# A Fourier filter and soft mixture of experts on one core: the first DFT stage with its operands swapped, its result kept in SBUF

## The chip, the core and the metric

The kernel runs on one core of one Trainium2 chip. A core has TensorE (PE in the profile; its weight loads are shown apart as PEld), VectorE (DVE), ScalarE (ACT), GpSimd (POOL) and SyncE (SP), whose queue here issues every DMA. The metric is the device time of one execution in microseconds (us). Before the change three runs took 440.77, 441.68 and 442.54 us, a median of 441.68 us. The profiled execution took 440.74 us; its span from the first to the last instruction of the program is 439.0 us.

## The reference

The input `x` holds 8 batches of 2496 rows of 256 float32 values. Each column of a batch is filtered in frequency, and all 19968 filtered rows then go through a soft mixture of 8 experts with 4 slots each. Cut to what is computed:

```python
X = np.fft.rfft(x, axis=1)
Y = X * (filt_r + 1j * filt_i)[None]
x = np.fft.irfft(Y, n=x.shape[1], axis=1).reshape(-1, 256)
logits = x @ phi                                  # 19968 x 32
d = softmax of logits down the columns            # over all rows
slot_input = d.T @ x                              # 32 x 256, 4 rows per expert
slot_out = relu(slot_input[e] @ w1[e]) @ w2[e]    # for each of the 8 experts
c = softmax of logits along the rows              # over the 32 slots
out = c @ slot_out                                # 19968 x 256
```

## The kernel before

A batch's DFT over 2496 = 39 x 64 points is done in two matrix stages. Row number s is written as 64 s1 + s2. The **first stage** sums over the 39 values of s1 with a small cosine and sine matrix `w1q`; three values of s2 share one matmul, so that 3 x 39 = 117 partitions are contracted and 3 x 40 = 120 numbers come out (20 residues t, a real and an imaginary part each). The **second stage** sums, for each t, over the 64 values of s2 and the two parts, 128 terms in all, and gives 64 frequencies.

*The first stage* (`s1_unit`, L271) holds `w1q` still in the array and streams the data past it, 512 columns (two groups of s2 by 256 columns of x) at a time, 11 units in a batch. For batch 0 that is one float32 matmul (L278). For the others `split_x` (L258) has ACT round the data to a short float32r value `xh` (L267) and POOL compute the remainder `xl` (L268), and three float32r matmuls replace the float32 one (L281): w1h by xh, w1l by xh, w1h by xl. The result has (j, q) on its partitions, but the second stage needs (s2, part) there. So ACT (DVE for some units of batch 0) copies it to `at` (L285, L283), a DMA writes it to `a_dram` in DRAM (L289), and `load_ash` (L299) reads it back in the other arrangement, 256 KB for two values of t.

*The second stage* (`x_unit`, L305) handles two values of t in one slot, 10 slots in a batch, 80 in all. It makes four matmuls with `ash` as the operand that stays, 128 rows by 128 columns, and 128 streamed columns of the table `b_t` (L312). DVE multiplies the result by the real and by the imaginary filter (L325, L326), DVE or POOL adds (L328), POOL subtracts (L329). `t_unit` (L333), two slots later, transposes the products on PE (L339) for ACT to copy into a `y` tile (L341). Every second slot it also multiplies by phi: eight matmuls with 32 columns of weights each, four of them standing side by side in the four column quarters of the array (L350).

*The rest.* After each group of batches (0 and 1, 2 and 3, 4 and 5, 6, 7) a `chain` (L363) computes the logits (an inverse DFT of the filtered products with phi, L383 to L430), their running maximum, the dispatch weights and their DFT (L461 to L527), and adds to the slot inputs with matmuls over the saved `y` tiles (L554). It is a Python generator, advanced by `hop`, two steps in each slot, and its matmuls, too, often use 32 columns in quarters of the array. After the last group come `psi` (L777), the experts (L789 to L815), and the output stage (L832 to L913), which scales and transposes the combine weights, multiplies them by the slot outputs and writes 20 MB to DRAM.

*What sets the order.* Each engine runs its own instructions in program order. The order in each engine's program is made at build time by a list scheduler from the order in which the code issues the work: in slot n the second stage of that slot, the first stage of units five slots ahead (`AHEAD`), the transposes of two slots back, two hops. All loads, the writes to `a_dram` among them, stand in SP's one queue. The order of the loads at the start is written by hand (`STEPS`, L59).

*PSUM* is eight banks of 2 KB per partition: two each for the first stage (`ps_s1`), the second (`ps_x`), the transposes (`ps_t`) and the chain (`ps_c`).

Of the kernel before, what the change touches and what calls it, by code (L numbers as in the profile page):

```python
# [19 lines left out]
NT = 20  # L20
NI = 22
NH = 11
PK = 3
KR = PK * N1
# [11 lines left out]
NSPILL = 2  # L36
OUT_ORDER = (4, 5, 0, 1, 2, 3, 6, 7)
# [3 lines left out]
XC = 4  # L41
XB = 3
AB = 5
AHEAD = 5
ASH = 5
LT = 2
HOPS = 2
RT = 1
PR = 2
FB = 1  # L50
WM = 3
MV = 4
PA = 6
YB = 34
WL = 5
SB = 2


STEPS = "IB P FC TC TC TC C XC C XC CC AA X - - - ATATAT"  # L59
# [19 lines left out]
def shape_constants():  # L79
# [27 lines left out]
    bm = bm.reshape(P, NT, P)  # L107
    be = np.zeros((2, N2, 2, 2, 2, 32))
    for h in range(2):
        sg = 1.0 if h == 0 else -1.0  # L110
        for m in range(32):
            ph = 2 * np.pi * (((m + h) * s2) % N2) / N2
            co, si = np.cos(ph), np.sin(ph)
            be[0, :, 0, 0, h, m] = co
            be[0, :, 0, 1, h, m] = -si
            be[0, :, 1, 0, h, m] = sg * si
            be[0, :, 1, 1, h, m] = sg * co
            be[1, :, 0, 0, h, m] = -sg * si
            be[1, :, 0, 1, h, m] = -sg * co
            be[1, :, 1, 0, h, m] = co  # L120
            be[1, :, 1, 1, h, m] = -si
    tw = 2 * np.pi * np.repeat(s2, 2)[:, None] * np.arange(NT)[None] / SEQ
    bt = np.concatenate([bm[:, 0], be[0].reshape(P, P), be[1].reshape(P, P), np.cos(tw), np.sin(tw)], axis=1)
    for t in range(1, NT):
        full = be[0].reshape(P, P) * np.cos(tw[:, t : t + 1]) + be[1].reshape(P, P) * np.sin(tw[:, t : t + 1])
        assert np.abs(full - bm[:, t]).max() < 1e-12
    bh = bm[:, 0, :].copy()
# [51 lines left out]
def filter_layout(filt, special_zero):  # L179

    idx = np.array([[[freq_of(t, h, m) or 0 for m in range(32)] for h in range(2)] for t in range(NT)])
    a = filt[idx.reshape(NT, 64)]
    a = np.ascontiguousarray(a.reshape(NT, 64, 2, P).transpose(3, 0, 2, 1))
    if special_zero:
        a[:, 0, :, 0] = 0
    return a.reshape(P, NT * 2 * 64)
# [3 lines left out]
def fft_soft_moe(ctx, tc, x, fr, fi, fny, phi, w1, w2, cst, w1q, bmat, out):  # L190
# [5 lines left out]
    ps_s1 = ctx.enter_context(tc.tile_pool(name="ps_s1", bufs=2, space=PSUM))  # L196
    ps_x = ctx.enter_context(tc.tile_pool(name="ps_x", bufs=2, space=PSUM))
    ps_t = ctx.enter_context(tc.tile_pool(name="ps_t", bufs=2, space=PSUM))
    ps_c = ctx.enter_context(tc.tile_pool(name="ps_c", bufs=2, space=PSUM))
# [3 lines left out]
    w1h = const.tile([KR, QP], F32R, name="w1h")  # L203
    w1l = const.tile([KR, QP], F32R, name="w1l")
    nc.vector.tensor_copy(w1h, w1q_t)
    nc.vector.tensor_tensor(out=w1l, in0=w1q_t, in1=w1h.bitcast(F32), op=ALU.subtract)

    cst_t = const.tile([P, CST.shape[1]], F32, name="cst_t")
    b_t = const.tile([P, NT, P], F32, name="b_t")
# [22 lines left out]
    x0_cm, x0p = open_pool("x0p", 6, "left")  # L232
    tabs_cm, tabs = open_pool("tabs", 1, "right")
    prod_cm, prod = open_pool("prod", 2, "right")
    proda_cm, proda = open_pool("proda", 3, "right")

    fr_t = tabs.tile([P, NT, 2, 64], F32, name="fr_t")
    fi_t = tabs.tile([P, NT, 2, 64], F32, name="fi_t")

    xv = x.rearrange("b (s1 s2) d -> b s1 s2 d", s2=N2)  # L240
# [3 lines left out]
    def load_x(b, c):  # L244
        pool = x0p if b == 0 else proda
        t = pool.tile([KR, XC, DIM], F32, tag="xt", name=f"xt{b}_{c}", bufs=6 if b == 0 else XB)
        i0 = c * XC
        n = min(XC, NI - i0)
        for j in range(PK):
            s0 = run_of(i0, j)  # L250
            sp.dma_start(t[j * N1 : (j + 1) * N1, 0:n, :], xv[b, :, s0 : s0 + n, :])
        xts[b, c] = t

    a_dram = {}

    xhl = {}

    def split_x(b, u):  # L258

        c, k = divmod(2 * u, XC)  # L260
        xs = xts[b, c][:, k : k + 2, :]
        if b < FB:
            xhl[b, u] = xs, None
            return
        xh = proda.tile([KR, 2, DIM], F32R, tag="xh", name=f"xh{b}_{u}", bufs=3)
        xl = proda.tile([KR, 2, DIM], F32R, tag="xl", name=f"xl{b}_{u}", bufs=3)
        act.copy(xh, xs)  # L267
        pool_e.tensor_tensor(out=xl, in0=xs, in1=xh.bitcast(F32), op=ALU.subtract)  # L268
        xhl[b, u] = xh, xl

    def s1_unit(b, u):  # L271
        if u == 0:
            a_dram[b] = scr.tile([N2, QR, DIM], F32, tag="a_dram", name=f"a_dram{b}")
        xh, xl = xhl.pop((b, u))
        ps = ps_s1.tile([QP, 2, DIM], F32, tag="s1", name=f"s1_{b}_{u}")
        at = proda.tile([QP, 2, DIM], F32, tag="at", name=f"at{b}_{u}", bufs=AB)
        if xl is None:
            pe.matmul(ps, w1q_t, xh, start=True, stop=True)  # L278
        else:
            for n, (w, xx) in enumerate(((w1h, xh), (w1l, xh), (w1h, xl))):  # L280
                pe.matmul(ps, w, xx, start=(n == 0), stop=(n == 2))  # L281
        if b == 0 and u % 2 == 1:
            dve.tensor_copy(at, ps)  # L283
        else:
            act.copy(at, ps)  # L285
        k0 = PK * 2 * u
        dma = sp.dma_start
        if u < NH - 1:
            dma(a_dram[b][k0 : k0 + 2 * PK].rearrange("(i j) q d -> (j q) i d", j=PK), at)  # L289
        else:  # L290
            dma(a_dram[b][k0 : k0 + PK].rearrange("j q d -> (j q) d"), at[:, 0, :])
            dma(a_dram[b][k0 + PK], at[0:QR, 1, :])
# [4 lines left out]
    ashs = {}  # L297

    def load_ash(b, c):  # L299
        t0 = 2 * c  # L300
        ash = prod.tile([P, 2, DIM], F32, tag="ash", name=f"ash{b}_{c}", bufs=ASH)
        sp.dma_start(ash, a_dram[b].rearrange("k (r t) d -> (k r) t d", t=NT)[:, t0 : t0 + 2, :])
        ashs[b, c] = ash

    def x_unit(b, c):  # L305

        t0 = 2 * c
        ash = ashs.pop((b, c))
        ps = ps_x.tile([P, 4, 2, 64], F32, tag="x", name=f"x_{b}_{c}")
        for k in range(2):  # L310
            for dh in range(2):
                pe.matmul(  # L312
                    ps[:, 2 * k + dh].rearrange("q r c -> q (r c)"),
                    ash[:, k, dh * P : (dh + 1) * P],
                    b_t[:, t0 + k, :],
                    start=True,
                    stop=True,
                )
        frv = fr_t[:, t0 : t0 + 2].rearrange("q p h (o c) -> q (p h) o c", o=1).broadcast_to([P, 4, 2, 64])
        fiv = fi_t[:, t0 : t0 + 2].rearrange("q p h (o c) -> q (p h) o c", o=1).broadcast_to([P, 4, 2, 64])  # L320
# [9 lines left out]
        if c == 0:  # L330
            dve.tensor_tensor(out=yt[:, 0:2, 1, 0], in0=ps[:, 0:2, 1, 0], in1=fny_t, op=ALU.mult)
# [302 lines left out]
    for c in range(6):  # L634
        load_x(0, c)
# [310 lines left out]
```

## Time and profile before

| what | value |
|---|---|
| median of three runs | 441.68 us (440.77 to 442.54) |
| profiled execution, its span | 440.74 us, 439.0 us |
| first and last matmul of the second stage (L312) | 35.4 us, 300.4 us |
| `psi`, with which the experts begin (L777) | 349.0 us |
| first output matmul, last output matmul (L885) | 371.7 us, 430.7 us |
| bytes moved by DMA | 107.01 MB |
| of these, `a_dram` written and read back | 21.0 MB and 21.0 MB |
| mean granted TensorE clock | 0.975 |

A row of a group names line, engine, operation, output and inputs, shapes and count; then the time during which at least one instruction of it ran, the mean of one in ns, and the idle time of the engine ahead of them. A row of the timeline gives the start, the length from first start to last end, and the count of like instructions. Matmuls overlap, so the pace of TensorE is the distance between starts, not the length. A float32 matmul of 128 columns stands in the trace as two instructions, each with a weight load; a transpose is one. A row by stretch of time gives the busy time of PE, PEld, DVE, ACT and POOL, then the granted clock, the share of the DMA engines and GB/s.

### The profile page before, as it was taken

Reading aid. Unit: us, or ns where it says so; the run is one execution under the profiler, and the core shown is the slowest. Engines: PE = TensorE matmul, PEld = TensorE weight load, DVE = VectorE, ACT = ScalarE, POOL = GpSimd, SP = SyncE. Lnnn points to the kernel's source line nnn. Section 1 sums busy time; section 2 is a strip of 40 time slices with the busy share of each in tenths; the row PEclk is TensorE's granted clock in tenths of the full one; section 3 lists DMA queues with packets and bytes.
Section 4 is the critical chain, followed back from the end, with each engine's and each line's share of the span. In section 5 each row is a group of like instructions: output and inputs, shape, how many; then the busy total and the mean of one; then the engine's idle time right before and its main releaser. Section 6 shows DMA issues by size and latency. Waiting matters only on the chain. (4 is left out here: it accounts for less than half of the span.)

```text
span 439.0 us, 12271 instructions
## 1 busy us (share of the span) xinstructions
PE 383.8 (87%) x4705; PEld 293.1 (67%) x4705; DVE 288.8 (66%) x571; ACT 235.9 (54%) x513; POOL 232.7 (53%) x290
## 2 busy tenths in 40 slices
PE   8658788897999899999998999999999699878882
PEld 3236565685978687887877688777767445667761
DVE  1336442794699983878999287896477324777882
ACT  2376546466676845775693333461454122766772
POOL 0029557687769564966876056572200103877880
PEclk9879999999999999999999999999998999998997
DMA  6999999989979969787995624332298992787897
GB/s 172 258 274 268 299 277 294 316 253 307 296 230 312 288 194 297 223 260 210 264 293 168 218 76 121 97 99 97 80 375 295 298 283 94 293 341 301 320 352 262
DMA packets 62683, 107.01 MB, mean 244 GB/s; under 512 B 7006, under 2 KB 38622, under 8 KB 61090
## 3 DMA queue, kind: packets, MB, share of 16 engines
q1 hardware_dynamic: 62626, 106.24, 76.7%
q8 instruction: 37, 0.61, 0.5%
q14 instruction: 20, 0.16, 0.1%
HBM read 63.48 MB, written 42.74 MB: 242 GB/s over the span
## 5 line engine op out<-in xcount | busy, mean ns | idle before, releaser
L268 POOL TENSOR_TENSOR xl<-xt,xh 117x512 fp32r<-117x512 f32 x77 | 103.4, 1352 | 61.9 <-ACT xh L267 57.1
L312 PE MATMUL x<-b_t,ash 128*128 128x128 f32 x640 | 89.6, 280 | 6.0 <-DMA ash<-a_dram 3.7
L312 PEld LDWEIGHTS x<-b_t,ash 128*128 128x128 f32 x640 | 80.0, 191 | 15.7 <-DMA ash<-a_dram 5.0
L325 DVE TENSOR_TENSOR yt<-x,fr_t 128x512 f32<-128x512 f32 x80 | 54.8, 685 | 53.9 <-PE x L312 49.9
L329 POOL TENSOR_TENSOR yt<-yt,t 128x256 f32<-128x256 f32 x80 | 65.5, 821 | 40.1 <-DVE t L326 28.3
L267 ACT CAST xh<-xt 117x512 fp32r<-117x512 f32 x77 | 47.0, 622 | 45.4 <-DMA xt<-in_x 22.0
L341 ACT COPY y<-t 128x512 f32<-128x512 f32 x80 | 46.4, 591 | 33.7 <-PE t L339 27.8
L852 POOL TENSOR_TENSOR cr<-c,cr 117x256 fp32r<-117x256 f32 (+1 forms) x48 | 32.1, 688 | 53.5 <-ACT cr L851 53.4
L285 ACT COPY at<-s 120x512 f32<-120x512 f32 x83 | 48.2, 587 | 21.0 <-PE s L278 9.3
L326 DVE TENSOR_TENSOR t<-x,fi_t 128x512 f32<-128x512 f32 x80 | 54.4, 680 | 0.0
L339 PE MATMUL t<-cst_t,yt 128*128 128x128 f32 x320 | 48.9, 276 | 2.3 <-POOL xl L268 1.9
L281 PE MATMUL s<-xh,w1h 117*120 117x512 f32 x77 | 35.9, 467 | 11.3 <-ACT xh L267 9.2
L328 DVE TENSOR_TENSOR yt<-yt,t 128x256 f32<-128x256 f32 x60 | 43.5, 731 | 0.8
L339 PEld LDWEIGHTS t<-cst_t,yt 128*128 128x128 f32 x320 | 37.3, 141 | 9.7 <-issue 3.3
L861 DVE CAST st<-ct 128x384 fp32r<-128x384 f32 (+1 forms) x112 | 32.6, 363 | 6.7 <-PE ct L855 6.4
L885 PE MATMUL out<-so,st 128*128 128x256 f32 (+1 forms) x160 | 30.1, 324 | 3.1 <-DVE st L861 2.9
L328 POOL TENSOR_TENSOR yt<-yt,t 128x256 f32<-128x256 f32 x20 | 16.2, 810 | 30.5 <-DVE t L326 24.2
L855 PE MATMUL ct<-cst_t,cr 117*128 117x117 f32 x176 | 26.0, 276 | 7.1 <-POOL cr L852 5.3
L281 PE MATMUL s<-xh,w1l 117*120 117x512 f32 x77 | 31.2, 405 | 1.0 <-issue 1.0
L281 PE MATMUL s<-xl,w1h 117*120 117x512 f32 x77 | 31.9, 421 | 0.0
L885 PEld LDWEIGHTS out<-so,st 128*128 128x128 f32 (+1 forms) x160 | 24.4, 217 | 8.2 <-DVE st L861 7.2
L350 PE MATMUL l<-yt,phi_t 128*32 128x128 f32 x640 | 26.9, 278 | 3.0 <-ACT y L341 2.7
(111 smaller groups left out, 579.1 us busy)
## 6 DMA issues: line engine op xcount, KB each, us to landing
ash<-a_dram SPq DMA_DIRECT2D x80, 256.0 KB
a_dram<-at SPq DMA_DIRECT2D x80, 240.0 KB
xt<-in_x SPq DMA_DIRECT2D x120, 156.0 KB
w<-in_w SPq DMA_DIRECT2D x64, 256.0 KB
out<-ob SPq DMA_DIRECT2D x12, 1024.0 KB
out<-ob SPq DMA_DIRECT2D x8, 512.0 KB
out<-obr SPq DMA_DIRECT2D x8, 448.0 KB
xt<-in_x SPq DMA_DIRECT2D x24, 78.0 KB
```

Source lines behind the costliest of these rows:

```text
L267: act.copy(xh, xs)
L268: pool_e.tensor_tensor(out=xl, in0=xs, in1=xh.bitcast(F32), op=ALU.subtract)
L281: pe.matmul(ps, w, xx, start=(n == 0), stop=(n == 2))
L285: act.copy(at, ps)
L312: pe.matmul(ps[:, 2 * k + dh].rearrange("q r c -> q (r c)"), ash[:, k, dh * P : (dh + 1) * P], b_t[:, t0 + k, :], start=True, stop=True,)
L325: dve.tensor_tensor(out=yt, in0=ps, in1=frv, op=ALU.mult)
L326: dve.tensor_tensor(out=t2, in0=ps[:, :, ::-1, :], in1=fiv, op=ALU.mult)
L328: add.tensor_tensor(out=yt[:, :, 1, :], in0=yt[:, :, 1, :], in1=t2[:, :, 1, :], op=ALU.add)
L329: pool_e.tensor_tensor(out=yt[:, :, 0, :], in0=yt[:, :, 0, :], in1=t2[:, :, 0, :], op=ALU.subtract)
L339: pe.transpose(pt[:, k, dh, :], yt[:, c % 2, 2 * k + dh].rearrange("q r c -> q (r c)"), ident)
L341: act.copy(y, pt.rearrange("k p h d -> k p (h d)"))
L885: nc.tensor.matmul(pr[0:rows, kk, :], lhs(k + kk), so, start=True, stop=True)
```

## The change

The first stage now holds the *data* still and streams `w1q` past it. The host lays x out for that: 117 partitions (three columns of x by the 39 values of s1, padded to 128), and 43 blocks of 128 columns, (64 values of s2) x (two halves `dh` of the 256 columns of x). One float32 matmul takes a block of x as its weights and streams the 120 columns of `w1q` (L246); its result has (dh, s2) on the 128 partitions. A unit is four blocks, again 11 units in a batch. ACT (DVE for the odd units of batch 0) copies a unit into a tile `a` of the batch with a rearrangement in the free dimension: neighbouring elements that it writes lie 512 bytes apart. `a_dram`, `at`, `ash`, the split into `xh` and `xl` and their instructions are gone.

In `a` the real and the imaginary part are no longer on different partitions, so the second stage contracts the 64 values of s2 and adds up the two parts in PSUM. Partitions 0 to 63 belong to the columns 0 to 127 of x, partitions 64 to 127 to the columns 128 to 255. A slot makes eight matmuls (six in the first slot of a batch) of 64 rows each, alternately on the upper and the lower half of the array's rows, the two halves writing to two PSUM banks:

```diff
-        for k in range(2):
-            for dh in range(2):
-                pe.matmul(ps[:, 2 * k + dh]..., ash[:, k, dh * P : (dh + 1) * P], b_t[:, t0 + k, :], start=True, stop=True)
+        for k in range(2):
+            t = t0 + k
+            for r in range(2 if t else 1):
+                for dh in range(2):
+                    h = slice(64 * dh, 64 * dh + 64)
+                    pe.matmul(ps[:, dh, k, 0]..., am[h, r * NT + t, :], bt_t[h, t, r ^ dh, :],
+                              start=(r == 0), stop=(r == 1 or t == 0))
...
-        add = pool_e if b >= PA else dve
-        add.tensor_tensor(out=yt[:, :, 1, :], in0=yt[:, :, 1, :], in1=t2[:, :, 1, :], op=ALU.add)
+        pool_e.tensor_tensor(out=yt[:, :, 1, :], in0=yt[:, :, 1, :], in1=t2[:, :, 1, :], op=ALU.add)
```

The first stage:

```diff
-        ps = ps_s1.tile([QP, 2, DIM], F32, tag="s1", name=f"s1_{b}_{u}")
-        at = proda.tile([QP, 2, DIM], F32, tag="at", name=f"at{b}_{u}", bufs=AB)
-        if xl is None:
-            pe.matmul(ps, w1q_t, xh, start=True, stop=True)
-        else:
-            for n, (w, xx) in enumerate(((w1h, xh), (w1l, xh), (w1h, xl))):
-                pe.matmul(ps, w, xx, start=(n == 0), stop=(n == 2))
...
-            dma(a_dram[b][k0 : k0 + 2 * PK].rearrange("(i j) q d -> (j q) i d", j=PK), at)
+        ps = ps_c.tile([P, GU, QP], F32, tag="c", name=f"s1_{b}_{u}")
+        for g in range(n):
+            pe.matmul(ps[:, g], xt[0:KR, g], w1q_t, start=True, stop=True)
+        src = ps.rearrange("p g (e q) -> p (g e) q", q=QR)[:, 0:nd]
+        dst = amps[b][:, :, d0 : d0 + nd].rearrange("p q d -> p d q")
+        if b == 0 and u % 2 == 1:
+            dve.tensor_copy(dst, src)
+        else:
+            act.copy(dst, src)
```

What goes with it:

- The second stage's PSUM tile takes two banks, so `ps_x` has four. The first stage has no banks of its own any more: it shares the two of `ps_c` with the chain.
- The table `bt_t` comes whole by DMA (2.6 MB); before, it was made on ACT and DVE from a small one (`build_b`, L594, L595). The filters are one array.
- `AHEAD` is 1 instead of 5, `HOPS` 3 instead of 2, one x tile of 256 KB is one DMA instead of three; the loads at the start are in plain order: all of x of batch 0, constants, tables for three slots, four units of x of batch 1.
- The POOL takes the additions of all batches (before, of batches 6 and 7).
- Three logit tiles instead of two are spilled to DRAM and read back. The batches are written out in the order 6, 7, 0 to 5 (before 4, 5, 0 to 3, 6, 7). The output stage copies 1024 columns at a time (before 512), out of three PSUM tiles of two banks.
- The experts' weights wait in other tiles: 2 loaded early, 20 after the last slot into `a` and the filter table, the rest into `y` and product tiles.

How this moves instructions on TensorE, first in the middle of a batch in which no chain runs. `x` is the second stage, `s` the first, `t` the transposes, `l` the product with phi. Before:

```order
L312 MATMUL x_3_913<-b_t,ash_3_705 128x128 x4
L281 MATMUL s_2_9_965<-xl_9_898,w1h 120x512
L339 MATMUL t_1_930<-cst_t,yt_0_800 128x128 x4
L312 MATMUL x_4_954<-b_t,ash_4_743 128x128 x4
L281 MATMUL s_2_10_972<-xh_10_905,w1h 120x512
L281 MATMUL s_2_10_972<-xh_10_905,w1l 120x512
L350 MATMUL l_0_938<-yt_0_800,phi_t 32x128 x8
L339 MATMUL t_2_980<-cst_t,yt_2_876 128x128 x4
```

and after, at the same kind of place:

```order
L268 MATMUL x_3_713<-bt_t,a_226 128x128 x8
L246 MATMUL s_2_4_727<-w1q_t,xt_4_595 128x120 x4
L296 MATMUL t_1_735<-cst_t,yt_0_623 128x128 x4
L307 MATMUL l_0_743<-yt_0_623,phi_t 32x128 x8
L268 MATMUL x_4_753<-bt_t,a_226 128x128 x8
L246 MATMUL s_2_5_768<-w1q_t,xt_5_635 128x120 x4
L296 MATMUL t_2_776<-cst_t,yt_2_693 128x128 x4
```

Before, only `l` uses a part of the array (a column quarter); `x`, `s` and `t` use all of it. Now `x`, with 64 rows, uses half of the rows, so the shape in use changes at every step but from `s` to `t`. Counted over TensorE's whole program the shape changes 154 times before and 370 times after; the matmuls of `x` stand in 117 unbroken runs, 42 of them with an odd count.

The second place is on TensorE where a chain (here that of batches 0 and 1) comes to its dispatch part, `u` (the DFT of the dispatch weights and its transposes) and `dt`. Before:

```order
L339 MATMUL t_3_2202<-cst_t,yt_2_2037 128x128 x2
L496 MATMUL u_0_0_1755<-cst_t,u_1575 128x128 x4
L496 MATMUL u_0_4_1761<-cst_t,u_1575 128x128 x4
L339 MATMUL t_3_2202<-cst_t,yt_2_2037 128x128 x2
L312 MATMUL x_6_2225<-b_t,ash_6_1961 128x128 x3
L350 MATMUL l_1_2209<-yt_2_2037,phi_t 32x128 x8
```

and after:

```order
L307 MATMUL l_4_1778<-yt_8_1588,phi_t 32x128 x8
L442 MATMUL u_0_1304<-cst_t,d_1284 32x60 x32
L246 MATMUL s_3_6_1339<-w1q_t,xt_6_1017 128x120 x4
L442 MATMUL u_4_1349<-cst_t,d_1284 32x60 x32
L442 MATMUL u_8_1401<-cst_t,d_1284 32x60 x20
L442 MATMUL u_8_1401<-cst_t,d_1284 32x20 x4
L461 MATMUL u_0_0_1444<-cst_t,u_1285 128x128 x4
L461 MATMUL u_0_4_1450<-cst_t,u_1285 128x128 x4
L246 MATMUL s_3_7_1456<-w1q_t,xt_7_1076 128x120 x4
```

Before, second-stage work and transposes of the running batch stand between the chain's steps. After, the batch's ten slots are through (`l_4` is its last), and between the chain's steps stand only first-stage units of the next batch, which use the same two PSUM banks. This goes on to the end of the chain, and the next batch's second stage begins behind it.

More of the change, by code (lines that the diff above doesn't have):

```diff
@@ L23 @@
 PK = 3
+ND = 43
+GU = 4
 KR = PK * N1
@@ L106, in shape_constants @@
     bm[:, 0, 0, 1, 0, 0] = np.cos(ph)
[L107 to L127, printed above, removed]
+    bm = bm.transpose(1, 0, 2, 3, 4, 5).reshape(2, N2, NT, P)
+    bt = np.stack([bm.reshape(P, NT, P), bm[::-1].reshape(P, NT, P)], axis=2).reshape(P, NT * 2 * P)
+    bh = bm.reshape(P, NT, P)[:, 0, :].copy()
     bh[:, 0] *= 0.5
@@ L242, in fft_soft_moe @@
+    even_cm, even = open_pool("even", 1, "right")
+    xs_cm, xs = open_pool("xs", XB, "right")
+    ft_t = tabs.tile([P, NT // 2, 2, 4 * 64], F32, name="ft_t")
     xts = {}
     def load_x(b, c):
[L245 to L251, printed above, removed]
@@ L252, in load_x @@
-        xts[b, c] = t
[L254 to L269, printed above, removed]
+        t = (x0p if b == 0 else xs).tile([P, GU, P], F32, tag="xt", name=f"xt{b}_{c}")
@@ L620, in fft_soft_moe @@
         at_slot.setdefault((b - 1) * CPB + min(u, CPB - 1) - AHEAD, []).append((b, u))
-    xnext = [(b, c) for b in range(1, BATCH) for c in range(6)]
+    xnext = list(units)
     def next_x():
@@ L673, in fft_soft_moe @@
     minv_t = work.tile([P, NT, KP * 2], F32, name="minv_t")
[L674 removed]
     for n in range(-AHEAD, 0):
[L676 removed]
         for b, u in at_slot.get(n, ()):
             s1_unit(b, u)
[L679 to L681 removed]
+            next_x()
+    late = list(range(TP, CPB))
     last = {bs[-1]: g for g, bs in enumerate(GROUPS)}
```

294 lines of the change are left out of this document (130 added, 164 removed).

## Prediction

> **What bounds the kernel now.** I read the page's first part, then its busy time by stretch, then the waits where TensorE is not full, then the timeline of TensorE for the price of single steps. The page:
>
> ```profile
> span 439.0 us, 12271 instructions
> PE 383.8 (87%) x4705; PEld 293.1 (67%) x4705; DVE 288.8 (66%) x571; ACT 235.9 (54%) x513; POOL 232.7 (53%) x290
> ```
>
> The stages follow from the first and last start of three lines (this view gives min/median/max in ns, then those starts): the first stage of batch 0 (L278), the second stage (L312), and `psi`, where the experts begin (L777).
>
> ```profile
> L278 PE MATMUL s<-xt,w1q_t x22: 590/593/1057, 6.9 to 23.4; 117*120 117x512 f32 x22
> L312 PE MATMUL x<-b_t,ash x640: 272/275/377, 35.4 to 300.4; 128*128 128x128 f32 x160
> L777 PE MATMUL psi<-repz,s_run x4: 276/276/297, 349.0 to 349.4; 128*128 128x32 f32 x4
> ```
>
> Busy time by stretch (PE, PEld, DVE, ACT, POOL, then granted clock, DMA share, GB/s) and PE's waits from 35 to 80 us:
>
> ```profile
> 20.00:40.00 20.00, 13.91 (x58) 9.52 (x57) 9.36 (x23) 13.68 (x33) 9.13 (x13) 0.80 0.92 273
> 40.00:60.00 20.00, 15.71 (x121) 11.79 (x120) 10.69 (x18) 10.37 (x22) 12.00 (x11) 1.00 0.96 296
> 60.00:80.00 20.00, 15.29 (x130) 11.08 (x129) 9.56 (x18) 11.40 (x23) 13.51 (x14) 1.00 0.94 283
> 100.00:300.00 200.00, 190.62 (x2814) 156.01 (x2815) 157.62 (x260) 116.85 (x247) 126.83 (x127) 1.00 0.72 218
> 300.00:350.00 50.00, 43.91 (x853) 33.10 (x854) 27.20 (x76) 19.43 (x52) 6.58 (x12) 0.97 0.71 235
> 320.00:330.00 10.00, 8.66 (x162) 6.22 (x160) 8.45 (x26) 5.95 (x19) 0.71 (x2) 1.00 1.05 381
> PE s L281 <- ACT xh L267: 4.0, 3, 1.8
> PE x L312 <- DMA ash<-a_dram: 3.7, 4, 1.6
> ```
>
> So there are three regimes. Up to 35 us the second stage waits for loads. From 40 to 80 us PE is idle 9.0 of 40 us while the DMA engines are 94 to 96% busy, and it waits for x and for `ash`. From 100 to 300 us PE is busy 190.6 of 200 us: there only PE's own work counts, and what is taken from POOL, ACT, DVE or DMA is worth nothing.
>
> **The change, part by part.** All against the profiled execution's 440.74 us, which lies 0.94 us under the median of the runs.
>
> *The start: -16.* Before the first second-stage matmul the new order needs, in SP's queue, x of batch 0 (2.82 MB), `w1q` and constants (0.12 MB), tables for three slots (1.57 MB) and the small tables (0.29 MB): 4.8 MB. The rates above, 296 and 381 GB/s, make that 16.2 and 12.6 us. The first first-stage matmul now stands at 6.9 us, after about half a MB; so loading begins near 4 us, and the tables are in at 16.6 to 20.2 us. The first stage of batch 0 runs beside it, since x stands ahead in the queue. I take 19.5 instead of 35.4: -16. At 273 GB/s and with two late copies it would be about 25 us (-10); at the fast end -19.
>
> *From 40 to 80 us: -9.* The trip through DRAM and the split into `xh` and `xl`, for which PE waits there, both go. With 256 KB per unit a batch needs 2.82 MB of x in some 33 us (265 us for 8 batches), well under the rates above. I take all 9.0 us; the bounds are 0 and -9.
>
> *First stage on PE: +8.* The timeline of before (start, length, then the group) around one unit and the product with phi:
>
> ```profile
> 202.67 0.39 PE L281 MATMUL s<-xh,w1h 117*120 117x512 f32 x1
> 202.90 0.39 PE L281 MATMUL s<-xh,w1l 117*120 117x512 f32 x1
> 203.13 0.40 PE L281 MATMUL s<-xl,w1h 117*120 117x512 f32 x1
> 203.46 0.62 PE L350 MATMUL l<-yt,phi_t 128*32 128x128 f32 x10
> ```
>
> Starts lie 0.23 us apart, so a unit is 0.69 us, 0.79 with the change to phi behind it; about 0.75 on average, and 77 units (batches 1 to 7) are 58 us. After, 301 float32 matmuls of 120 columns replace them. Their price is that of the second stage's float32 matmuls of 128 columns:
>
> ```profile
> 277.72 0.60 PE L339 MATMUL t<-cst_t,yt 128*128 128x128 f32 x4
> 278.16 1.06 PE L312 MATMUL x<-b_t,ash 128*128 128x128 f32 x8
> 279.14 0.65 PE L350 MATMUL l<-yt,phi_t 128*32 128x128 f32 x16
> 279.72 1.16 PE L312 MATMUL x<-b_t,ash 128*128 128x128 f32 x8
> 280.71 0.60 PE L339 MATMUL t<-cst_t,yt 128*128 128x128 f32 x4
> ```
>
> Eight instructions (four matmuls, one slot) take 0.98 us to the next group's start, of which 0.09 belongs to the change of shape (below): 0.89, or 0.223 us a matmul. 301 x 0.223 = 67, hence +9, less 1 for 120 columns instead of 128: +8. Bounds +2 (all of it scaled by 120/128 and the dearer old unit of 0.79) and +13.
>
> *Second stage on PE: +3.* Before, 80 slots x 0.89 = 71. After, 624 matmuls of 64 rows. If the two halves run side by side, as the four column quarters of L350 do above (16 instructions in 0.58 us, where one by one they would take 16 x 0.111 = 1.78), a pair costs 0.223: 312 x 0.223 = 70. The 42 odd runs add half a pair each, 42 x 0.11 = 5. No row of before shows row halves side by side; if they do not, 624 x 0.223 = 139 (rival A).
>
> The Trainium skill ("TensorE: Matmul & The Clock Gate", Part 3) says that small row tiles run at once but measured four of them at 3.07 times one, not 4. By that efficiency the second stage would be an estimated 70 / 0.77 = 91 us and the total 16 us above mine.
>
> *Changes of shape: +30.* This is the largest term. The dense rows give the price. Leaving a shape: ahead of L350 the last of L312's eight has 0.98 - 7 x 0.111 = 0.20 us instead of 0.11, so +0.09. Entering a matmul with 128 weight columns from the quarters: the second L312 group takes 0.99 us with a change to transposes behind it that is none of shape, so +0.10. Transposes from the quarters cost less:
>
> ```profile
> 311.10 0.65 PE L350 MATMUL l<-yt,phi_t 128*32 128x128 f32 x16
> 311.67 0.66 PE L339 MATMUL t<-cst_t,yt 128*128 128x128 f32 x4
> 312.16 0.27 PE L383 MATMUL ltr<-cst_t,lt 128*128 128x128 f32 x1
> ```
>
> 0.49 us for four instead of 0.44: +0.05. That 64 rows count as another shape is seen at L416, the only one of before:
>
> ```profile
> 316.65 0.60 PE L339 MATMUL t<-cst_t,yt 128*128 128x128 f32 x4
> 317.18 0.85 PE L416 MATMUL v<-cst_t,v 64*120 64x64 f32 x11
> 317.96 0.64 PE L350 MATMUL l<-yt,phi_t 128*32 128x128 f32 x16
> ```
>
> 0.53 us from L339 to L416 instead of 0.44: again +0.09. The order of the instructions has 216 more changes than before: 117 into the row halves at 0.09 + 0.10 (22.8 us), out of them 53 to matmuls at the same 0.195 (10.3), 56 to transposes at 0.15 (8.3) and 8 to quarters at 0.12 (0.9); 7 more from full to quarters (0.8); and 25 of the way back from the quarters (45 to matmuls, 32 to transposes before, 27 and 25 now) that are no more, -4.5. Sum 38.7 us, 0.18 a change. Of all changes 47 fall into the three stretches in which only a chain and first-stage units run; there PE waits anyway. That leaves 169 of 216: 30 us. Bounds: 0 if row halves don't pay what L416 pays, 20 if only the leaving is paid (216 x 0.093), 45 if entering rows costs both halves' loads.
>
> The Trainium skill ("TensorEngine Tiling (Array Packing)", Key Properties) says that changing the tiling mode drains TensorE. By the drain alone it would be an estimated 20 us; the trace has 0.10 us more where 128 weight columns follow, and I go by the trace.
>
> *New waits: +17.* Three of the chains (batches 0 and 1, 2 and 3, 4 and 5) now have their dispatch part alone with first-stage units. Its steps come one after another through other engines:
>
> ```profile
> L461 DVE TENSOR_TENSOR d<-lg,m_run 117x512 f32<-117x512 f32 x6 | 7.4, 1278 | 0.0
> L462 ACT ACTIVATE d<-d 117x512 f32<-117x512 f32 x6 | 3.8, 631 | 0.0
> L497 DVE COPY u<-u 128x512 f32<-128x512 f32 x8 | 5.4, 680 | 1.3 <-PE u L496 1.3
> L517 ACT COPY dt<-dt 128x512 f32<-128x512 f32 x8 | 4.7, 584 | 9.4 <-PE dt L510 9.4
> ```
>
> For one chain two or three of each (shorter ones counted by their share): about 3.8 + 1.8 + 1.8 + 1.6 = 9 us. Behind the waiting matmul on PE stand first-stage units, which cannot pass it, and behind those the next batch's second stage. I take half as covered: 4 us a chain, 12 for three. Covered now by second-stage work, its cost is 0 there. The last chain, batch 7 alone, has less beside it than in 300 to 350 us, where PE was idle 6.1 us: +5. Bounds 0 and 30.
>
> *At nothing.* Other engines, by their groups:
>
> ```profile
> L268 POOL TENSOR_TENSOR xl<-xt,xh 117x512 fp32r<-117x512 f32 x77 | 103.4, 1352 | 61.9 <-ACT xh L267 57.1
> L329 POOL TENSOR_TENSOR yt<-yt,t 128x256 f32<-128x256 f32 x80 | 65.5, 821 | 40.1 <-DVE t L326 28.3
> L285 ACT COPY at<-s 120x512 f32<-120x512 f32 x83 | 48.2, 587 | 21.0 <-PE s L278 9.3
> L861 DVE CAST st<-ct x112: 149/240/869, 369.1 to 429.4; 128x384 fp32r<-128x384 f32 x40, 128x84 fp32r<-128x84 f32 x40, 128x64 fp32r<-128x64 f32 x16, 128x14 fp32r<-128x14 f32 x16
> ```
>
> POOL loses 103 us and gains 60 additions x 0.82 = 49. The first stage's copy now writes with 512-byte steps; the nearest row is L861, whose largest casts, scattered too, take up to 0.87 us for 384 elements. So 0.6 to 1.1 us for a copy of 480, at most 97 us of ACT in 440. Each engine stays below its 87% PE. Experts and output stage: 0, from -7 to +9.
>
> Sum: -16 - 9 + 8 + 3 + 30 + 17 = +33, so **474 us**.
>
> **Rivals.** *A: the halves don't run side by side.* Then 65 us come on top, 539 us. For it: no row of before shows two row tiles at once, and each half still loads 128 weight columns, the long kind of load:
>
> ```profile
> L312 PEld LDWEIGHTS x<-b_t,ash 128*128 128x128 f32 x640 | 80.0, 191 | 15.7 <-DMA ash<-a_dram 5.0
> L350 PEld LDWEIGHTS l<-yt,phi_t 128*32 128x32 f32 x640 | 15.4, 109 | 13.0 <-ACT y L341 5.3 <-issue 4.8 <-ACT at L285 0.8
> ```
>
> Against it: quarters of the array do run four at once, and the alternation of the halves is written out. Chance 0.10.
>
> *B, the other side: row halves cost no change of shape.* The 0.09 us ahead of L416 may be its wait for a copy of ACT, not the shape, and then weights for the free half could load while the other works. Only the 7 changes between full and quarters remain (+1), and with half of the new waits (8.5): -16 - 9 + 8 + 3 + 1 + 8.5 = -4.5, 436 us; with all of them 445, with none 428. It decides for a gain where changes and new waits together stay below 14 us, for instance 0.065 us for each of the 216 and no wait. Against it: +0.09 on both sides of L416. Chance 0.22.
>
> *C: the two shared banks hold the loop.* If one in three of the 77 units waited 0.6 us for a chain's copy to give its bank back, that is 25 x 0.6 = +15, 489 us. For it: chain and first stage had two banks each. Against it: a slot is 3.3 us (265 for 80), a unit's matmuls and copy under 2. Chance 0.08, inside the main range.
>
> **How the numbers follow.** The main case has 0.60. Its own range, with the cheap ends (changes 20, waits 5, first stage +2) and the dear ends (changes 40, waits 30, first stage +13, half of the 40-to-80 gain), is about 446 to 514. To hold 8 in 10 it must reach into B, to 434; A and the lower part of B are left out. What can be told from no change is 0.5%, 2.2 us. Faster than that (below 438.5) is B without most waits: 0.17. Within it 0.05, the rest of B near the break-even. Slower: 0.78.
>
> **What would show it.** The first second-stage matmul near 19.5 us. In dense parts the sixteen instructions of a slot's second stage about 0.9 us plus the changes; 1.8 says A. About 0.1 us more at the last matmul of each shape and ahead of each full-array matmul: if the steps from `x` to `s` lie 0.11 us apart as within a group, B holds. PE idle in the three stretches with a chain alone, 4 us each, and for the last chain; waits of `s` for a copy on ACT or DVE say C. `psi` near 382. The forecast is wrong in its main step if PE's work between first and last second-stage matmul is not some 40 us more (8 + 3 + 30).

## The result and the profile after

The changed kernel takes 490.79 us (median of four runs, 490.03 to 492.26) against 441.63 us before: 1.112 times as long, interval 1.108 to 1.115. The forecast was 474 us with a range of 434 to 514. The profiled execution took 490.03 us, 49.3 us more than that of before.

The page's first part, and first and last start of the first stage (L246), the second stage (L268) and `psi` (L709) after the change:

```profile
span 488.2 us, 13497 instructions
PE 435.4 (89%) x5748; PEld 338.7 (69%) x5748; DVE 242.1 (50%) x476; ACT 221.8 (45%) x391; POOL 165.8 (34%) x273
L246 PE MATMUL s<-w1q_t,xt x688: 274/275/569, 6.9 to 335.0; 117*128 117x120 f32 x172
L268 PE MATMUL x<-bt_t,a x1248: 272/272/373, 20.1 to 360.0; 64*128 64x128 f32 x179
L709 PE MATMUL psi<-repz,s_run x4: 276/276/297, 398.3 to 398.6; 128*128 128x32 f32 x4
```

POOL is busy 67 us less than before, DVE 47 less, DMA moves 70 MB instead of 107. The time does not follow them: TensorE is busy 51.6 us more, and the time grew by 49.3. Busy time by stage, cut at the first and last second-stage matmul and at `psi`, first before (PE, PEld, DVE, ACT, POOL, clock, DMA share, GB/s):

```profile
0.00:35.40 35.40, 24.03 (x55) 11.35 (x55) 10.10 (x28) 15.00 (x35) 5.53 (x11) 0.86 0.85 238
35.40:300.40 265.00, 245.42 (x3260) 198.54 (x3261) 197.93 (x323) 154.50 (x322) 173.49 (x171) 1.00 0.77 234
300.40:349.00 48.60, 42.84 (x841) 32.13 (x839) 26.57 (x74) 19.43 (x52) 6.18 (x12) 0.96 0.71 237
```

then after:

```profile
0.00:20.10 20.10, 17.74 (x100) 13.43 (x100) 5.58 (x7) 6.88 (x7) 0.20 (x4) 1.00 0.88 301
20.10:360.00 339.90, 319.93 (x4566) 254.66 (x4567) 166.41 (x287) 156.75 (x269) 112.60 (x161) 0.99 0.25 75
360.00:398.30 38.30, 27.83 (x536) 21.02 (x534) 18.70 (x51) 13.22 (x38) 5.44 (x10) 0.91 0.98 340
```

The start is 15.3 us shorter, the second stage's stretch 74.9 us longer, the last chains 10.3 us shorter (the chain of batch 6 now lies ahead of 360 us), the rest the same. From the first second-stage matmul to `psi` TensorE is busy 347.8 instead of 288.3 us (+59.5) and idle 30.4 instead of 25.3 (+5.1). Ahead of it, it is busy 6.3 us less and idle 9.0 us less (2.4 instead of 11.4).

TensorE's timeline in the middle of a batch (start, length, group):

```profile
59.80 1.16 PE L268 MATMUL x<-bt_t,a 64*128 64x128 f32 x16
60.89 1.15 PE L246 MATMUL s<-w1q_t,xt 117*128 117x120 f32 x8
61.88 0.60 PE L296 MATMUL t<-cst_t,yt 128*128 128x128 f32 x4
62.41 1.16 PE L268 MATMUL x<-bt_t,a 64*128 64x128 f32 x16
63.50 1.15 PE L246 MATMUL s<-w1q_t,xt 117*128 117x120 f32 x8
64.49 0.60 PE L296 MATMUL t<-cst_t,yt 128*128 128x128 f32 x4
65.02 0.65 PE L307 MATMUL l<-yt,phi_t 128*32 128x128 f32 x16
```

Sixteen instructions of `x` take 1.09 us: eight steps of 0.11 with two instructions starting 6 or 7 ns apart in each, plus 0.2 for the two changes. `s` takes 0.99 (eight steps and 0.10 for entering), `t` 0.53 ahead of `x` (0.44 and 0.09 for leaving). No gap is left between any of them.

### The profile page after: what moved, and what is told of

Its sections match the earlier page's. It is cut to its first block, busy times and chain, and to the rows that moved or that the text cites. A ratio compares the mean times of both kernels' runs of the same rounds, so it can differ in the third digit from the quotient of the medians.

```text
span 488.2 us, 13497 instructions
## 1 busy us (share of the span) xinstructions
PE 435.4 (89%) x5748; PEld 338.7 (69%) x5748; DVE 242.1 (50%) x476; ACT 221.8 (45%) x391; POOL 165.8 (34%) x273
## 4 chain that ended last, share of the span: by engine, by line
PE 70%; DVE 13%; DMA 5%; ACT 5%; issue 3%; POOL 2%; SPq 1%; DVEq 0%; ACTq 0%
PE x L268 17%; PE s L246 15%; PE t L296 7%; PE l L307 4%; PE out L819 4%; PE s L519 4%; DMA xt<-in_x 3%; PE v L354 3%; PE lg L386 2%; PE u L442 2%; DMA ft_t<-in_ft 2%; PE ct L790 2%; ACT a L252 2%; PE dt L475 2%; DVE ob L823 2%
## 5 line engine op out<-in xcount | busy, mean ns | idle before, releaser
L285 POOL TENSOR_TENSOR yt<-yt,t 128x256 f32<-128x256 f32 x80 | 58.3, 729 | 242.3 <-DVE t L284 216.0
L252 ACT COPY a<-s 128x480 f32<-128x480 f32 (+1 forms) x83 | 79.7, 974 | 102.3 <-PE s L246 102.3
L283 DVE TENSOR_TENSOR yt<-x,ft_t 128x512 f32<-128x512 f32 x80 | 55.1, 689 | 104.5 <-PE x L268 104.5
L268 PE MATMUL x<-bt_t,a 64*128 64x128 f32 x1248 | 105.5, 289 | 1.3 <-DVE yt L288 1.1
L246 PE MATMUL s<-w1q_t,xt 117*128 117x120 f32 x688 | 97.4, 287 | 3.2 <-DVE u L462 1.0
L268 PEld LDWEIGHTS x<-bt_t,a 64*128 64x128 f32 x1248 | 83.2, 187 | 22.0 <-issue 15.5
L246 PEld LDWEIGHTS s<-w1q_t,xt 117*128 117x128 f32 x688 | 83.8, 193 | 17.2 <-issue 3.9
L286 POOL TENSOR_TENSOR yt<-yt,t 128x256 f32<-128x256 f32 x80 | 59.7, 746 | 0.0
L284 DVE TENSOR_TENSOR t<-x,ft_t 128x512 f32<-128x512 f32 x80 | 54.4, 680 | 0.0
L307 PE MATMUL l<-yt,phi_t 128*32 128x128 f32 x640 | 30.7, 280 | 0.0
L790 PE MATMUL ct<-cst_t,cr 117*128 117x117 f32 x176 | 25.3, 270 | 5.4 <-DVE st L796 2.6
L821 ACT COPY ob<-out 128x1024 f32<-128x1024 f32 x22 | 22.0, 1015 | 11.7 <-PE out L819 11.7
L790 PEld LDWEIGHTS ct<-cst_t,cr 117*128 117x128 f32 x176 | 18.4, 141 | 10.4 <-POOL cr L787 9.8
L307 PEld LDWEIGHTS l<-yt,phi_t 128*32 128x32 f32 x640 | 16.6, 109 | 11.4 <-issue 10.6
```

The source lines that it names most:

```text
L246: pe.matmul(ps[:, g], xt[0:KR, g], w1q_t, start=True, stop=True)
L252: act.copy(dst, src)
L268: pe.matmul(ps[:, dh, k, 0].rearrange("q r c -> q (r c)"), am[h, r * NT + t, :], bt_t[h, t, r ^ dh, :], start=(r == 0), stop=(r == 1 or t ...
L283: dve.tensor_tensor(out=yt, in0=px, in1=frv, op=ALU.mult)
L284: dve.tensor_tensor(out=t2, in0=px[:, :, ::-1, :], in1=fiv, op=ALU.mult)
L285: pool_e.tensor_tensor(out=yt[:, :, 1, :], in0=yt[:, :, 1, :], in1=t2[:, :, 1, :], op=ALU.add)
```

## The experiments

Times of experiments are medians. Beside them the kernel before took 441.1 to 442.5 us, depending on the chip, and each ratio is to its runs on the same chip.

### What a change of shape costs

**Full rows.** The second stage without its row halves:

```diff
-            for r in range(2 if t else 1):
-                for dh in range(2):
-                    h = slice(64 * dh, 64 * dh + 64)
-                    pe.matmul(ps[:, dh, k, 0]..., am[h, r * NT + t, :], bt_t[h, t, r ^ dh, :], ...)
+            for r in range(2):
+                pe.matmul(ps[:, r, k, 0]..., am[:, r * NT + t, :], bt_t[:, t, r, :], start=True, stop=True)
```

> The second stage of the changed kernel with four matmuls of all 128 rows in a slot instead of eight of 64 (the sums over the two halves of the columns get mixed; it still streams the same number of columns one after another, 0.89 us a slot). Its order has 174 changes of shape instead of 370. Theory (each change costs TensorE 0.09 us on leaving and 0.10 us on entering full-width weights): 196 x 0.18 = 35 us less, and 5 us less for the 42 odd runs that are gone: 451 us (443 to 460). Rival (the time went into the shared banks and the chain's waits, changes are hidden): 484 to 491 us.

Measured: 463.7 us, ratio 1.050 (1.045 to 1.054); 27 us less than the changed kernel, where the theory had 40 and the rival 0 to 7. Its timeline, where `x`, `s` and `t` have one shape:

```profile
64.68 0.60 PE L294 MATMUL t<-cst_t,yt 128*128 128x128 f32 x4
65.12 1.06 PE L266 MATMUL x<-bt_t,a 128*128 128x128 f32 x8
66.01 1.05 PE L246 MATMUL s<-w1q_t,xt 117*128 117x120 f32 x8
66.90 0.60 PE L294 MATMUL t<-cst_t,yt 128*128 128x128 f32 x4
```

The same streams take 0.89, 0.89 and 0.44 us, without the 0.10 and 0.09 at each border. Added up over the span (the distance from each matmul's start to the next one's, idle time taken out), `x` takes 75.7 instead of 97.0 us, `t` 37.9 instead of 44.9, `s` 84.3 instead of 87.6, `l` 24.6 instead of 26.5: 33.5 us. Idle time, with the last matmul's latency ahead of it, is 66.0 instead of 59.5 us: with less work on TensorE more of its waits come to light, so 33.5 us of work are worth only 27 us of time. Some 3 us of the 33.5 belong to the odd runs (an estimate: 42 of them at 0.11 us, less 8 full matmuls at 0.223 that this version streams more, since it has four in the first slot of a batch too). The other 30.7 us for 196 changes make 0.16 each, not 0.18.

**Pairs.** The real computation, with two slots issued together:

```diff
-    for n in range(NS + LT):
+    for n0, n1 in zip(starts, starts[1:]):       # two slots each
+        for n in (n0, n0 + 1): x_unit(...)
+        for n in (n0, n0 + 1): hop(); s1_unit(...); hop()
+        for n in (n0, n0 + 1): t_unit(...)
```

> The changed kernel with the slots issued in pairs: two slots of second stage, then their two units of first stage, then two transposes. Same work; 295 changes of shape instead of 370, 52 odd runs instead of 42. Theory (0.18 us a change, 0.11 an odd run): -13.5 + 1 = 478 us (474 to 483). Rival (changes hidden, the waits decide; in pairs DVE is behind, and the transposes wait): 489 to 500 us.

Measured: 476.3 us, ratio 1.079 (1.075 to 1.083), 2 us below the theory. Two units of `s` and two of `t` now have one border:

```profile
54.56 2.04 PE L246 MATMUL s<-w1q_t,xt 117*128 117x120 f32 x16
56.44 1.04 PE L296 MATMUL t<-cst_t,yt 128*128 128x128 f32 x8
57.41 1.60 PE L268 MATMUL x<-bt_t,a 64*128 64x128 f32 x22
```

So 75 changes fewer, with the same matmuls, are worth 14.5 us (12.1 between the two profiled executions), 0.16 to 0.19 each: a second experiment gives the same price.

### Whether the halves run side by side

```diff
-        for k in range(2):
-            for r in range(2 if t else 1):
-                for dh in range(2):
+        for dh in range(2):
+            for k in range(2):
+                for r in range(2 if t else 1):
```

> The changed kernel with the eight matmuls of a slot ordered by half: first all four of the upper 64 rows, then all four of the lower. Same work, same order otherwise, same 370 changes. Theory (halves run side by side only because they alternate; TensorE is the bound): a slot's second stage takes 1.78 us instead of 0.89, with the odd runs 65 us more: 556 us (545 to 562). Rival (TensorE finds the free half by itself, or is not the bound): 491 to 500 us.

Measured: 524.4 us, ratio 1.188 (1.184 to 1.192), 34 us more than the changed kernel: between the two.

```profile
61.45 1.71 PE L268 MATMUL x<-bt_t,a 64*128 64x128 f32 x16
63.09 1.15 PE L246 MATMUL s<-w1q_t,xt 117*128 117x120 f32 x8
```

A slot takes 1.64 us here, not 1.09 and not 1.98 (sixteen steps and the two changes). In the starts one by one there are three pairs, 4 to 6 ns apart, in the middle of the sixteen; the first four and the last five instructions stand alone. Sixteen instructions thus take 13 steps of 0.11 us and the two changes. The records don't name the half. If a pair is one instruction of each half, TensorE begins the second half some three instructions ahead of its turn, so its matmuls don't start strictly in program order here. The halves do run side by side, and the alternation that the change writes out is worth 34 us.

### The shared banks and the chain

**One bank each.**

```diff
-    ps_c = pool("ps_c", bufs=2)
+    ps_c = pool("ps_c", bufs=1)
+    ps_s = pool("ps_s", bufs=1)      # the first stage
...
+        pool, tag = (ps_c, "c") if b == 0 and u % 2 else (ps_s, "s")     # batch 0 uses both
```

> The changed kernel with one PSUM bank for the first stage alone and one for the chain, instead of two that they share. The order now spreads the chain's first steps among second-stage slots; stretches of a chain without second stage remain, somewhat shorter, 352 changes of shape instead of 370. Theory (the shared banks hold the first stage back behind the chain, and TensorE idles 6 to 8 us in each of three stretches): half of these 20 us and 3 us of changes go: 478 us (470 to 483). Rival (the chain's own steps through other engines are what is waited for; with one bank they are slower): 489 to 497 us.

Measured: 518.8 us, ratio 1.176 (1.172 to 1.181): worse than the rival. The chain's matmuls, each now behind the copy out of its only bank, leave TensorE idle, and in these stretches the granted clock falls (seventh column of numbers, 0.83 and 0.77):

```profile
300.00:350.00 50.00, 38.32 (x575) 27.38 (x576) 24.75 (x44) 14.43 (x30) 10.36 (x14) 0.83 0.08 26
350.00:430.00 80.00, 60.25 (x838) 41.26 (x831) 30.58 (x77) 21.73 (x55) 10.96 (x18) 0.77 0.56 191
```

So this run doesn't answer its question; it shows that two shared banks are worth more than one for each.

**Two banks each.** The second stage's product fills only half of each of its banks, so two slots can share a tile and two banks become free:

```diff
-        ps = ps_x.tile([P, 2, 2, 2, 2, 64], ...)                       # bufs=2, index 3 always 0
+        if c % 2 == 0:
+            xps[0] = ps_x.tile([P, 2, 2, 2, 2, 64], ...)               # bufs=1, index 3 is c % 2
...
-        ps = ps_c.tile([P, GU, QP], F32, tag="c", ...)
+        ps = ps_s.tile([P, GU, QP], F32, tag="s", ...)                 # ps_s: two banks
```

> The changed kernel with two PSUM banks for the first stage alone and two for the chain; the second stage's two slots share two banks instead of having two each, so that a slot waits for DVE to be done with the one before it. 317 changes of shape instead of 370 and 18 odd runs instead of 42, worth -12 us. Theory (the shared banks are a cause of the three stretches with a chain alone): half of their 20 us of idle time goes too, 469 us (463 to 475). Rival (the chain's steps and the y tiles it holds make the stretches, whatever the banks): 476 to 482 us; and with a new wait of the second stage for DVE in each slot (0.3 us) 490 to 500.

Measured: 482.4 us, ratio 1.097 (1.090 to 1.104), the rival's time, and 8.4 us less than the changed kernel, where the fewer changes and odd runs alone were put at 12. The waits say why (engine, line, what it waited for, us in total, times, longest). In the changed kernel:

```profile
PE t L296 <- POOL yt L286: 6.9, 7, 1.8
PE dt L475 <- ACT a L252: 2.5, 3, 0.8
PE dd L491 <- ACT a L252: 1.9, 3, 0.6
```

and with the banks apart:

```profile
PE x L274 <- DVE t L290: 7.2, 9, 1.1
PE t L302 <- POOL yt L292: 4.0, 9, 0.8
```

The chain's `dt` and `dd` no longer wait for a bank that the first stage's copy `a` on ACT holds, which was 4.4 us. Between first and last second-stage matmul the idle time ahead of `dt`, `dd`, `z`, the transposes of `u` and the slot sums (L519) goes from 8.0 us to nothing. That is not the banks alone: with the banks apart the scheduler also puts slots of the second stage and transposes between these steps, so that no stretch without the second stage is longer than 6.4 us, where the changed kernel has three of 28 to 30 us. In place of these waits the second stage waits for DVE, 8.8 us instead of 1.1, since two slots share a tile, and the matmuls of `u` and `ltr` wait 7.1 us for ACT instead of 1.9. The theory was right on the cause of part of the idle time, and the time didn't show it because new waits took its place.

**Pairs and banks apart**: the same, in pairs, with all sixteen matmuls ahead of DVE's four multiplications.

> The banks apart as in the run before this, and the slots issued in pairs: sixteen second-stage matmuls in one run, then DVE's four multiplications, beside two units of first stage and two transposes. 246 changes of shape instead of 370, 66 runs instead of 117, 18 odd. Theory (0.18 us a change, 0.11 an odd run): -22 - 3 us, and half of the 20 us of idle time: 456 us (448 to 464). Rival (a pair waits for DVE's four multiplications of the pair before, 2.75 us, and gives back 0.5 us in 40 pairs): 470 to 480 us.

Measured: 470.0 us, ratio 1.067 (1.061 to 1.074): at the rival's lower end. The wait for DVE stays (`PE x L274 <- DVE t L294`, 6.5 us).

### The start

**Later tables.**

```diff
+    for _ in range(XB): next_x()
     load_tables(0)
...
-    for _ in range(XB): next_x()
```

> The changed kernel with the first four units of x of batch 1 (1 MB) loaded ahead of the tables instead of behind them; the order on TensorE is the same in every row. At 300 GB/s the first second-stage matmul comes 3.5 us later, at 23.6 us. Theory (what counts at the start is TensorE's idle time, and it has no other work ready there): 3.5 us later at the end, 494 us (492 to 495.5). Rival (the start is hidden behind later waits): 490 to 491.5 us.

Measured: 490.3 us, ratio 1.115 (1.108 to 1.122), the rival's time, but not for its reason. The first second-stage matmul stands at 20.0 us in spite of the 1 MB ahead of the tables: the tables were not what it waited for. The timeline of the changed kernel shows what was:

```profile
6.86 2.16 PE L246 MATMUL s<-w1q_t,xt 117*128 117x120 f32 x16
9.19 2.06 PE L246 MATMUL s<-w1q_t,xt 117*128 117x120 f32 x16 [0.17 <-ACT a L252]
11.41 2.07 PE L246 MATMUL s<-w1q_t,xt 117*128 117x120 f32 x16 [0.16 <-ACT a L252]
13.63 6.55 PE L246 MATMUL s<-w1q_t,xt 117*128 117x120 f32 x46 [0.15 <-ACT a L252]
20.11 0.94 PE L268 MATMUL x<-bt_t,a 64*128 64x128 f32 x12
```

Two units take 2.22 us, because a bank is free again only after a copy of 0.98 us.

**The copy twice**, as the copy's price:

```diff
+            act.copy(dst, src)
             act.copy(dst, src)
```

> The changed kernel with each of ACT's first-stage copies made twice (0.97 us more for ACT per unit, 83 units, and the PSUM bank is held that much longer). The order has 340 changes of shape instead of 370, worth -5 us. Theory (the copy is covered): 486 us (484 to 489). Rival (the two shared banks hold the loop through this copy): 495 to 520 us.

Measured: 499.5 us, ratio 1.135 (1.129 to 1.141), inside the rival's range. Between 26 and 100 us TensorE is busy 73.5 of 74 us: beside running slots the doubled copy is covered. It costs at the start, where the first second-stage matmul comes at 25.3 us instead of 20.1:

```profile
6.86 2.01 PE L246 MATMUL s<-w1q_t,xt 117*128 117x120 f32 x16
10.04 2.04 PE L246 MATMUL s<-w1q_t,xt 117*128 117x120 f32 x16 [1.17 <-ACT a L253]
13.25 2.04 PE L246 MATMUL s<-w1q_t,xt 117*128 117x120 f32 x16 [1.17 <-ACT a L253]
```

and in the stretches of a chain, where `u` now waits 4.1 us for the copy `a` on ACT.

**Four banks at the start.**

```diff
-        ps = ps_c.tile(...)
+        pool, tag = (ps_t, "t") if b == 0 and u % 4 > 1 else (ps_c, "c")
+        ps = pool.tile(...)
```

> The changed kernel with four PSUM banks instead of two for the first stage of batch 0 (the two of the transposes, idle then, beside the shared two). 366 changes of shape instead of 370. Theory (at the start the copies through two banks set the pace, 2.2 us for two units, and the tables are in before that): the units follow at TensorE's pace of 0.9 us, the first second-stage matmul is at 17.7 us instead of 20.1, 487.5 us (486.5 to 489). Rival (the tables land near 20 us and hold it): first matmul at 20 us, 490 to 491 us.

Measured: 491.4 us, ratio 1.115 (1.109 to 1.121). The first stage of batch 0 did speed up, and another wait was next:

```profile
6.16 9.76 PE L247 MATMUL s<-w1q_t,xt 117*128 117x120 f32 x86
18.38 1.38 PE L247 MATMUL s<-w1q_t,xt 117*128 117x120 f32 x8 [2.46 <-DMA xt<-in_x]
19.68 1.65 PE L269 MATMUL x<-bt_t,a 64*128 64x128 f32 x12
```

Its 86 instructions are through at 15.9 us. Then the first unit of batch 1, which stands ahead of the second stage in TensorE's order, waits until 18.4 us for its x, which is loaded behind the tables. The start is held by the banks and, 1.7 us earlier, by the loads.

**All of it**: pairs, banks apart, four banks at the start.

> Pairs and banks apart as before, with four banks for the first stage of batch 0 too. If the start's gain adds up: 470 - 2 = 468 us (466 to 470).

Measured: 464.9 us, ratio 1.050 (1.044 to 1.056), 3 us below what was expected, and the fastest version of the changed kernel that computes the result; it is still slower than the kernel before.

### The same price in the kernel before

`b_fewer_y` is the kernel before with `YB = 32`; `b_phi_in_twos` also holds back the products with phi and keeps three `yt` tiles for it instead of two:

```diff
-            pl = ps_t.tile(...)                      # eight matmuls, every second slot
+            l_todo.append((b, i))
+            if len(l_todo) == 2 or (b in last_b and c == CPB - 1):
+                l_units()                            # sixteen matmuls, every fourth slot
```

> The kernel before with 32 y tiles instead of 34, a control for the next run. 154 changes of shape as in the kernel before. 441 to 442 us if the two tiles don't matter; 443 to 446 if transposes wait for a free y tile while a chain holds them.

Measured: 446.3 us, ratio 1.011 (1.005 to 1.016): the two y tiles are worth about 1%. What waits for them is not shown.

> The kernel before, with 32 y tiles, and the products with phi issued for two pairs of slots together instead of for each (the last of a group alone): 138 changes of shape instead of 154. Theory (a change costs the same 0.1 to 0.2 us in the kernel before, and TensorE is its bound): 16 x 0.2 = 3 us less than the control, 438 us. Rival (it is hidden, or holding the products back makes the chain later): the control's time or more.

Measured: 455.0 us, ratio 1.030 (1.024 to 1.035): 9 us more than the control. TensorE is idle 64.3 us of its span, where the kernel before has 55.2. The products' own waits for ACT's y copies are hardly longer (3.5 instead of 2.7 us), so they are not the reason. The rival holds; which of the delays counts stays open, and so does what a change of shape costs the kernel before. No version of the changed kernel that computes the result beats the kernel before.

## Why the prediction was right

The direction, the bound and the mechanisms held; the size came out 16 us short, and the range was wide enough to hold that. By its own steps:

- **TensorE's own work** was forecast at 8 (first stage) + 3 (second stage) + 38.7 (all changes of shape) = 49.7 us. Counted as in the run with full rows, the first stage takes 87.6 instead of 72.4 us, `x` 97.0 instead of 73.6, `t` 44.9 instead of 36.4, `l` 26.5 instead of 22.8: 50.8 us more. The price of a change is 0.09 on leaving and 0.10 on entering, as read off the dense rows; the experiments give 0.16 to 0.19 each. The chain's other matmuls (`u`, `ltr`, `lg`) were put at nothing and take about 4 us more.
- **Which of it counts** was the step that failed. I took 47 changes (8.7 us) off the 216, as lying in the three stretches with a chain alone, where TensorE waits anyway. But the 216 are what the change adds, and nearly all of them are borders of the second stage (117 in, 117 out), which doesn't run in those stretches. Counted in the trace after, the stretches (119.8 to 149.1, 213.4 to 243.6 and 307.7 to 336.1 us) hold 53 changes, and only the first and the last of each border on the second stage. The other 47 are the chain's own, within it and against first stage and transposes; they are in the count of 370, but not in what the change adds, since the kernel before has this chain too. There was nothing to take off. The forecast's own sign was that its main step is wrong if TensorE's work between first and last second-stage matmul is not some 40 us more. It is 74.5 more there (the chain of batch 6 now lies ahead of the last one), and 59.5 more up to `psi`, where 41 were forecast: 8.7 us are these changes, the rest the chain's matmuls, the transposes of the next point and some 3 us in the four groups.
- **The start, -16**, had the right number for the wrong reason, by luck. The first second-stage matmul came at 20.1 us (19.5 forecast), but held by two banks and a copy of 0.98 us, with the loads close behind. And the 15.3 us were not all won. TensorE was idle for 9.0 of them and busy for 6.3. The transposes of the tables and one unit of batch 1 now stand behind the first second-stage matmul, where they take 2.7 and about 1.0 us; the forecast had no term for this. The rest, some 2.6 us, went because the same work ran slower before, at a granted clock of 0.86 in this stage and of 0.53 at its end:

```profile
30.00:35.00 5.00, 4.81 (x17) 3.31 (x16) 0.00 (x0) 2.01 (x6) 4.09 (x7) 0.53 0.87 246
```

- **40 to 80 us, -9**, held: TensorE is busy throughout, so the waits for x and `ash` are gone.
- **New waits, +17**, came near: in each stretch with a chain alone, 100 to 150, 200 to 250 and 300 to 350 us, TensorE is idle 6.4, 5.6 and 7.6 us. That is nearly all of its idle time between first and last second-stage matmul, 20.0 us; the kernel before had 10.6 there outside of 40 to 80 us, so 9.4 us are new (12 forecast). Behind the last second-stage matmul 4.7 us are new (5 forecast). In the stretches between, it has no idle time at all:

```profile
100.00:150.00 50.00, 43.63 (x685) 31.88 (x674) 24.88 (x41) 21.98 (x39) 8.91 (x12) 1.00 0.17 51
150.00:200.00 50.00, 50.00 (x694) 42.29 (x692) 23.37 (x39) 23.70 (x39) 21.22 (x30) 1.00 0.30 84
```

- **At nothing**: the copy with 512-byte steps is 0.97 us (0.6 to 1.1 forecast) and is covered beside slots, as the doubled copy shows, but not at the start and not where a chain shares its banks. The row below has 79.7 us of ACT for it:

```profile
L252 ACT COPY a<-s 128x480 f32<-128x480 f32 (+1 forms) x83 | 79.7, 974 | 102.3 <-PE s L246 102.3
```

- **Rival A** fell: two starts 7 ns apart at every 0.11 us, and 34 us more where the halves don't alternate. The Trainium skill ("TensorE: Matmul & The Clock Gate", Part 3) has four row tiles at 3.07 times one, by which the second stage would have been dearer; here two halves of 64 rows run at twice one, and the measurement decides.
- **Rival B** fell with full rows and pairs: row halves pay for the change of shape. The trace of before could have told more than I took from it, since L416 is not the only such place. `mb` (L447, 32 rows) stands in dense rows at 137.7, 217.6 and 285.6 us, and TensorE takes 0.09 us more ahead of it each time. The Trainium skill's drain ("TensorEngine Tiling (Array Packing)", Key Properties) fits the 0.09 us on leaving; the 0.10 on entering comes on top of it.
- **Rival C** is true in part: in the stretches with a chain alone 4.4 us of waits were for the first stage's copy out of a shared bank, and with the banks apart the stretches themselves went. The time didn't show it, since new waits took their place.

In short, from the first second-stage matmul to `psi` TensorE's work was 18.5 us more than forecast, its idle time 2.9 us less, and that matmul came 0.7 us later: 16.3 us in all, between 473.7 and the 490.0 of the profiled execution. The largest single part, 8.7 us, is the changes that should not have been taken off.

## What to carry to other kernels

On an engine that is busy more than 90% of the time, price an edit by that engine's own instructions alone, the borders between unlike matmuls among them: 216 borders of 0.16 to 0.19 us cost more here than a 42 MB trip through DRAM and 67 us of GpSimd work gave back. If a stage must use another array shape, group its matmuls; two slots in one run gave back 14 us. When a cost is priced by a difference of counts, take off only what is in that difference. And an earlier start is worth the distance by which it moves less the work that only moves behind it, here 15.3 less some 3.7 us.

## What the runs showed of the hardware

- Matmuls on two halves of 64 rows each start within 7 ns of each other, if they alternate; issued half after half, sixteen take 1.64 us, not 1.09 or 1.98, which fits a second half that begins some three instructions early.
- A change of array shape costs 0.09 us on leaving and 0.10 on entering a shape with 128 weight columns, for row halves as for column quarters.
- In two stretches in which TensorE idled a quarter of the time, its granted clock was 0.83 and 0.77 (one bank each), so that the work between the waits ran slower too. The share alone doesn't decide: from 60 to 80 us before, with 24% idle, the clock was 1.00.
- An ACT copy of 480 elements out of PSUM takes 0.97 us when it writes at 512-byte steps; one of 512 elements written in order took 0.59.
